# Four plain products after each piece of the first batch's attention, in a fused attention and two-layer kernel

## The chip, the cores and the metric

The kernel runs on one core of one Trainium2 chip. The metric is the device time of one execution in microseconds (us). Before the change three runs took 918.08, 918.32 and 920.32 us; the median is 918.32 us.

The engines named below are PE (TensorE, matrix products), PEld (its weight loads), DVE (VectorE), ACT (ScalarE), POOL (GpSimd) and SP (which issues the DMAs). Each engine works through its own instructions strictly in the order in which they stand.

## The reference: what is computed

```python
def _attn_ref(q, k, v):                     # 4 batches, 8 heads, 576 tokens, 64 columns
    scores = scale * np.matmul(q, k.transpose(0, 1, 3, 2))
    mask_local = (rel >= 0) & (rel < stride)                      # stride = 32, heads 0 to 3
    mask_strided = (rel >= 0) & (pos[None, :] % stride == pos[:, None] % stride)   # heads 4 to 7
    ...
    attn = np.exp(scores)
    attn = attn / (np.sum(attn, axis=-1, keepdims=True) + 1e-09)
    return np.matmul(attn, v).astype(np.float32)

def reference(**kwargs):
    attn_out = _attn_ref(**attn_kwargs)
    x = np.ascontiguousarray(attn_out.transpose(0, 2, 1, 3)).reshape(B * S, H * D)   # 2304 x 512
    x = _moe_ref(x=x, **moe_kwargs)         # g = s * relu(x @ w_in) ** 2 + b;  g @ w_out
    return _moe2_ref(x=x, **moe2_kwargs)    # g = h * cos(h), h = x @ w_in;     g @ w_out
```

Both layers go from 512 to 2048 columns and back. Their weights come as float64.

## The kernel before, in words

**Attention.** The masks leave few keys for each query, so the scores of one head fit one PSUM bank. Such a bank is an *item*. Each of the four batches has ten: four pairs of heads with two heads each ("loc" for the local heads, "str" for the strided), and two "rem" items for the tokens left over. An item passes these steps: a bf16 product of the identity with the mask puts the mask in the bank (L296), float32 products of q and k are added to it (L300), DVE takes the row maximum (L318, L319), ACT takes the exponentials (L343), DVE normalises (L356 to L358), PE transposes the result (L366), ACT copies the transposes out (L374), PE multiplies by the values (L398, two items together), and ACT and DVE write the product as two parts `xhi` and `xlo` (L109, L112).

`Attention.micro` hands this out piece by piece: values of a finished pair, transposes of the item three places back, scores of the next item. Each `next(steps)` gives one piece. `LOADS` says at which item the next operands are loaded.

**The two layers.** Every product of x with w_in and of g with w_out is three products of parts (L521, L575, L578), since the operands are split in a high and a low part. Weights are converted from float64 on DVE in small steps (`convert_ops`, L128 to L140) by `bg_step`. The first four weight tiles, `wearly`, come by DMAs that stand in the opening list of loads (`FIRST`).

**Order.** The program text is not the order on an engine. A scheduler that works at compile time puts each engine's instructions in order, with the text's order as priority: what its own reckoning takes to be ready may go ahead of what still waits. Around the change the loop is `while not att.batch_done(0)`: one piece of attention, one step of everything under way (`tick`), and 0.6 steps of weight conversion. From the third item's values on it also issues the first products of layer one.

**Banks.** PSUM has eight banks: one for "h", four for "acc", three for "att". In the first batch scores use "acc", transposes use "att" and the values' products use "h", until the first layer's products take "h" over. `dummy` is one of the three "att" banks. Before the change 18 products of zeros (L629) write it at the program's start and nothing reads it.

Of the kernel before, what the change touches and what calls it, by code (L numbers as in the profile page):

```python
# [27 lines left out]
LG, LK = 64, 96  # L28
# [18 lines left out]
ALAG = 3  # L47
# [18 lines left out]
ACT_SB = 8  # L66
PRE = 3
WARM = 18
NP0 = NC * NT - NPB * 512
PE_MASK = 2  # L70
QKW = 544
# [10 lines left out]
def net(ctx, tc, qk, vloc, vstr, w1, w2, s, b, out):  # L82
    nc = tc.nc
# [27 lines left out]
    def split_lo(dst_lo, src, hi):  # L111
        nc.vector.tensor_tensor(dst_lo, src, hi.bitcast(F32), ALU.subtract)  # L112

# [1 line left out]
    wtile, ready = {}, set()  # L115

    def convert_ops(raws, dst, key):
        """Rebias the exponent by a product, shift the top 29 + 3 mantissa bits into place, add the sign."""
        tmp = st_p.tile([P, 512], F32, tag="st", name="wtmp")
        ops = []  # L120
        o = 0
        for raw in raws:
            n = raw.shape[1]
            t = tmp[:, o : o + n]
            tu = t.bitcast(U32)
            lo32, hi32 = raw[:, :, 0], raw[:, :, 1]
            o += n
            ops.append(lambda t=t, h=hi32: nc.vector.tensor_scalar(t, h.bitcast(F32), 2.0**-112, None, ALU.mult))  # L128
            ops.append(lambda tu=tu: nc.vector.tensor_scalar(tu, tu, 3, None, ALU.logical_shift_left))
            ops.append(  # L130
                lambda tu=tu, l=lo32: nc.vector.scalar_tensor_tensor(  # L131
                    tu, l, 29, tu, ALU.logical_shift_right, ALU.bitwise_or
                )
            )
            ops.append(
                lambda tu=tu, h=hi32: nc.vector.scalar_tensor_tensor(  # L136
                    tu, h, 0x80000000, tu, ALU.bitwise_and, ALU.bitwise_or
                )
            )
        ops.append(lambda: split_hi(dst[:, 0, :], tmp))  # L140
        ops.append(lambda: split_lo(dst[:, 1, :], tmp, dst[:, 0, :]))
        ops.append(lambda: ready.add(key))
        return ops
# [16 lines left out]
    bg_due = [0.0]  # L160

    def bg_step(n):
        """Run n operations, or the fraction that is due, of the work that waits in the background."""
        bg_due[0] = min(bg_due[0] + n, 4.0)
        while bg_due[0] >= 1 and (bg_now or bg):
            if not bg_now:
                bg_now.extend(bg.pop(0)())
            bg_now.pop(0)()
            bg_due[0] -= 1

    def weight(n, k):
        """The tile, with the work that fills it issued."""
        while (n, k) not in ready:
            bg_step(1)
        return wtile[n, k]
# [5 lines left out]
            stages.append(gen)  # L181

    def tick():
        """One step of everything that is under way, the oldest first."""
        for g in list(stages):
            if next(g, "end") == "end":
                stages.remove(g)

    def w_job(n, k):
        """Loads run at once; the arithmetic follows in small steps."""  # L190
        raws = []
        for c in range(2):
            raw = st_p.tile([P, 256, 2], U32, tag="st", name="wraw")
            nc.sync.dma_start(out=raw, in_=w_src(n, k, 256 * c, 256 * (c + 1)))
            raws.append(raw)
        return convert_ops(raws, w_alloc(n, k), (n, k))

# [1 line left out]
    qk_t, v_t, rem_t = {}, {}, {}  # L199

    def load_qk(bb, hp):
# [37 lines left out]
        rem_t[bb].append(rv)  # L239

    class Item:
        """A bank of scores: `parts` are (partitions, keys, tiles, first column) and `mms` fill them."""

        def __init__(self, bb, hp, j, kind):
            self.bb, self.hp, self.j, self.kind = bb, hp, j, kind
# [14 lines left out]
                o += m * n  # L260

        def score_mms(self):
            """(partition, column, queries, keys) of each product, by part."""
            r = slice(self.j * D, (self.j + 1) * D)
            if self.kind == "rem":
                rq = rem_t[self.bb][0]
                yield 0, [(LG * hp, 0, rq[r, hp, 0, 0:LG], rq[r, hp, 1, :]) for hp in range(2)]
                res = []
                for hp in range(2):
                    rs = rem_t[self.bb][1]  # L270
                    res.append((0, LK + hp * SR, rs[r, hp, 0, :], rs[r, hp, 1, :]))
                yield 1, res
                return
            t = qk_t[self.bb, self.hp]
            res = []
            for i in range(4):
                if self.kind == "loc":
                    for g in range(2):
                        o = (2 * i + g) * LG
                        res.append((g * LG, i * LK, t[r, 0, o : o + LG], t[r, 1, o : o + LK]))  # L280
                else:
                    o = i * SG
                    res.append((0, i * SG, t[r, 0, o : o + SG], t[r, 1, o : o + SG]))
            yield 0, res
# [91 lines left out]
                    eng.tensor_copy(dst, src)  # L376

        def pv_mms(self, o):
            """Products of one head with its values; the other head of the pair fills the other columns."""
            dst = o[self.j * D : (self.j + 1) * D]  # L380
            dc = slice(self.j * D, (self.j + 1) * D)
            if self.kind == "rem":
                rv = rem_t[self.bb][2]
                res = []
                for hp in range(4):
                    m, k, c = (LG, LK, hp * LG) if hp < 2 else (SR, SR, P + (hp - 2) * SR)
                    res.append((dst[:, c : c + m], rv[:k, hp, dc], self.pt[:k, c : c + m]))
                return res
            v = v_t[self.bb, self.hp]
            m, k, n = (LG, LK, 8) if self.kind == "loc" else (SG, SG, 4)  # L390
            return [
                (dst[:, i * m : (i + 1) * m], v[:k, i, dc], self.pt[:k, i * m : (i + 1) * m]) for i in range(n)
            ]
# [39 lines left out]
        it.stored = True  # L433

    class Attention:
        """All heads' score banks in one pipeline: scores at step i, transposes at i + ALAG, values one step later."""

        def __init__(self):
            self.items = []
# [13 lines left out]
            return self.items[i] if 0 <= i < len(self.items) else None  # L453

        def batch_done(self, bb):
            """Whether the batch's last values have been written."""
            return self.items[10 * bb + 9].stored

        @property
# [1 line left out]
            return self.n > len(self.items) + ALAG  # L461

        def micro(self):
            """The pipeline's pieces: values of a pair that is done, transposes, scores."""
            while not self.done:
                i = self.n
                new, old, done = (self.item(i - k) for k in (0, ALAG, ALAG + 1))
                if done and done.j == 1:
                    while not done.moved:
                        tick()  # L470
                    spawn(run_values(self.item(i - ALAG - 2), done, self.tags[2]))
                    yield
                if old:
                    while not old.ready:
                        tick()
                    spawn(old.run_transp(self.tags[1], self.alloc))
                    yield
                if new:
                    spawn(new.run_scores(self.tags[0], new.bb < PE_MASK, self.alloc))
                bb, k = divmod(i, 10)  # L480
                for what, b_, hp in LOADS.get(k, ()):
                    if 0 < bb + b_ < B:
                        {"qk": load_qk, "v": load_v}[what](bb + b_, hp)
                if k == 9 and 0 < bb + 1 < B:
                    load_rem_qk(bb + 1)
                if k == 3 and 0 < bb < B:
                    load_rem_v(bb)
                self.n += 1
                if new:
                    yield  # L490

# [1 line left out]
    PER = NBLK * FP  # L493
    NSLOT = 2 * NPASS * PER
    h_ps, g_t, acc = {}, {}, {}
# [1 line left out]
    acc_n = [None]  # L497

    def acc_bank():
        """Two of attention's banks join the four of the accumulators when it is done."""  # L500
        if acc_n[0] is None:
            return psum("acc", "acc")
        acc_n[0] += 1
        return psum("acc" if (acc_n[0] - 1) % 6 < 4 else "att", "acc")

    def h_bank(t):
        """Attention's third bank joins the one of h."""
        return psum("h" if acc_n[0] is None or t % 2 == 0 else "att", "h_ps")

    def slot(t):  # L510
# [109 lines left out]
        )  # L620
    nc.vector.tensor_copy(identb, ident)

    # products of zeros keep the tensor engine's clock up until the first operands are there
    zeros = part[:, NP0 + (NPB - 1) * 512 : NP0 + NPB * 512 - 256]
    nc.vector.memset(zeros, 0.0)
    warm = zeros.bitcast(BF16)
    dummy = psum("att", "dummy")
# [18 lines left out]
    early = 0  # L646
    while not att.batch_done(0):
        next(steps)
        tick()
        bg_step(EARLY_BG)  # L650
        if early < 2 and att.items[PRE + 2 * early].stored:
# [99 lines left out]
```

## Time and profile before

| | |
|---|---|
| three runs, median | 918.32 us |
| profiled execution, first to last instruction (span) | 916.2 us |
| median of the runs less that span | 2.1 us |
| PE busy | 906.8 us (99%) |
| DVE busy | 581.8 us (64%) |
| ACT busy | 464.9 us (51%) |
| DMA, share of 16 engines' span | 18.5% |
| mean granted TensorE clock | 0.987 of full speed |

The profile gives the profiled execution by its span alone; what lies around the span is the 2.1 us by which the runs' median is longer. The granted clock has two levels here, 1.2 GHz (0.50) and 2.4 GHz (1.00). Times in the rows count from the span's start. A matmul's end is modelled, so neighbouring ones overlap in the timeline, and the distance between two starts says more than a duration. In the chain of waits a piece lasts from the end of the piece before it.

### The profile page before, as it was taken

How to read it: one execution, taken by the hardware profiler on the slowest of the kernel's cores; microseconds unless marked ns; L12 is line 12 of the kernel's file. 1: busy time of each engine (PE TensorE's matmuls, PEld its weight loads, DVE VectorE, ACT ScalarE, POOL GpSimd, SP SyncE). 2: the span in 40 equal slices, each digit the busy share in tenths (PEclk: the TensorE clock that was granted, in tenths of full speed). 3: DMA queues.
4: the chain of work that ended last, by engine and by line, in shares of the span. 5: the costliest groups of instructions: out<-in, count | busy, mean ns of one | idle time of the engine just before them, and what ended most of it. 6: DMA issues, size and time to landing. Idle time of an engine off the chain costs nothing.

```text
span 916.2 us, 12761 instructions
## 1 busy us (share of the span) xinstructions
PE 906.8 (99%) x4834; PEld 736.1 (80%) x4834; DVE 581.8 (64%) x1399; ACT 464.9 (51%) x1053; POOL 4.0 (0%) x15
## 2 busy tenths in 40 slices
PE   8999999999999999999999999999999999999998
PEld 4777777788888888888888888888888888888887
DVE  3598898448633883358646994479646974564444
ACT  3587977545333443344445654455445544454443
POOL 1000000000000000000000000000000000000000
PEclk8699999999999999999999999999999999999999
DMA  9446452002100230012100120013000220001111
GB/s 243 122 147 184 145 152 77 1 24 92 70 1 0 70 116 1 1 45 94 46 1 24 58 95 10 0 58 104 24 1 24 92 70 1 1 1 47 46 47 69
DMA packets 41486, 54.97 MB, mean 60 GB/s; under 512 B 7632, under 2 KB 21200, under 8 KB 41424
## 3 DMA queue, kind: packets, MB, share of 16 engines
q1 hardware_dynamic: 41424, 54.15, 18.5%
q8 instruction: 38, 0.62, 0.3%
q14 instruction: 24, 0.20, 0.1%
HBM read 49.42 MB, written 4.72 MB: 59 GB/s over the span
## 4 chain that ended last, share of the span: by engine, by line
PE 96%; DMA 2%; DVE 1%; SPq 0%; ACT 0%; issue 0%
PE h_ps L521 43%; PE acc L575 22%; PE acc L578 22%; PE s_ps L300 4%; PE o_ps L398 2%; PE t_ps L366 2%; DMA wearly<-in_w_dram 1%; PE s_ps L296 0%; DMA wraw<-in_w_dram 0%; SPq L208 0%; DVE wtmp L131 0%; DVE wtmp L128 0%; DVE wtmp L136 0%; DVE part L358 0%; SPq L219 0%; DVE part L592 0%
## 5 line engine op out<-in xcount | busy, mean ns | idle before, releaser
L521 PE MATMUL h_ps<-xhi,w 128*128 128x512 f32 (+1 forms) x1280 | 396.4, 373 | 0.6 <-DVE r L552 0.4
L521 PEld LDWEIGHTS h_ps<-xhi,w 128*128 128x128 f32 x1280 | 233.7, 188 | 45.4 <-DVE r L552 1.0
L521 PE MATMUL h_ps<-xlo,w 128*128 128x512 f32 (+1 forms) x640 | 236.1, 369 | 0.0
L575 PE MATMUL acc<-gh,w 128*128 128x512 f32 (+1 forms) x640 | 201.6, 376 | 0.0
L578 PE MATMUL acc<-w,gh 128*128 128x512 f32 x576 | 181.1, 395 | 0.0
L109 ACT ACTIVATE gh<-r 128x512 fp32r<-128x512 f32 (+1 forms) x160 | 94.1, 588 | 103.6 <-DVE r L552 52.7
L521 PEld LDWEIGHTS h_ps<-xlo,w 128*128 128x128 f32 x640 | 120.6, 188 | 21.4
L575 PEld LDWEIGHTS acc<-gh,w 128*128 128x128 f32 x640 | 116.8, 188 | 22.8 <-issue 0.7
L112 DVE TENSOR_TENSOR gl<-r,gh 128x512 fp32r<-128x512 f32 (+1 forms) x160 | 101.5, 634 | 48.1 <-ACT gh L109 42.7
L578 PEld LDWEIGHTS acc<-w,gh 128*128 128x128 f32 x576 | 107.3, 188 | 23.9 <-ACT gh L109 0.4
L575 PE MATMUL acc<-gl,w 128*128 128x512 f32 (+1 forms) x320 | 118.9, 372 | 0.0
L578 PE MATMUL acc<-w,gl 128*128 128x512 f32 x288 | 113.5, 394 | 0.0
L535 ACT ACTIVATE r<-h_ps 128x512 f32<-128x512 f32 (+1 forms) x80 | 44.1, 551 | 115.8 <-PE h_ps L521 115.4
L548 DVE SCALAR_TENSOR_TENSOR r<-a,r 128x512 f32<-128x512 f32 (+1 forms) x80 | 50.8, 635 | 71.9 <-ACT a L546 71.8
L592 DVE TENSOR_TENSOR part<-acc,part 128x512 f32<-128x512 f32 (+1 forms) x114 | 72.3, 656 | 31.9 <-PE acc L575 19.0
L541 DVE TENSOR_SCALAR r<-r,sb 128x512 f32<-128x512 f32 (+1 forms) x72 | 37.0, 514 | 80.1 <-ACT r L536 80.1
L545 ACT ACTIVATE r<-h_ps 128x512 f32<-128x512 f32 (+1 forms) x80 | 44.4, 555 | 78.6 <-PE h_ps L521 78.3
L550 ACT ACTIVATE r<-r 128x512 f32<-128x512 f32 (+1 forms) x80 | 47.2, 590 | 61.5 <-DVE r L548 61.3
L575 PEld LDWEIGHTS acc<-gl,w 128*128 128x128 f32 x320 | 60.2, 188 | 10.5
L552 DVE TENSOR_TENSOR r<-h_ps,r 128x512 f32<-128x512 f32 (+1 forms) x80 | 50.8, 634 | 27.1 <-ACT r L550 26.8
L578 PEld LDWEIGHTS acc<-w,gl 128*128 128x128 f32 x288 | 54.3, 189 | 13.0 <-DVE gl L112 0.2
L109 ACT ACTIVATE w<-wtmp 128x512 fp32r<-128x512 f32 x64 | 40.0, 626 | 24.6 <-DVE wtmp L136 20.7
(66 smaller groups left out, 776.5 us busy)
## 6 DMA issues: line engine op xcount, KB each, us to landing
wraw<-in_w_dram SPq DMA_DIRECT2D x120, 256.0 KB, 3.1
out_dram<-part SPq DMA_DIRECT2D x18, 256.0 KB, 2.0
qk<-in_qk_dram SPq DMA_DIRECT2D x8, 544.0 KB, 3.9
v<-in_vloc_dram SPq DMA_DIRECT2D x8, 384.0 KB, 4.0
qk<-in_qk_dram SPq DMA_DIRECT2D x6, 504.0 KB, 4.9
wearly<-in_w_dram SPq DMA_DIRECT2D x4, 512.0 KB
v<-in_vstr_dram SPq DMA_DIRECT2D x6, 252.0 KB
part<-in_qk_dram SPq DMA_DIRECT2D x2, 504.0 KB
```

The costliest lines, as they stand in the source:

```text
L109: nc.scalar.activation(dst_hi, src, AF.Copy)
L112: nc.vector.tensor_tensor(dst_lo, src, hi.bitcast(F32), ALU.subtract)
L521: nc.tensor.matmul(h_ps[t][:, :tb], wt[:, wi, c * P : (c + 1) * P], xt[:, c, t0 : t0 + tb], start=(c == 0 and i == 0), stop=(c == NC - 1 a ...
L535: nc.scalar.activation(r, h, AF.Relu)
L541: nc.vector.tensor_scalar(r, r, sb[:, 0:1], sb[:, 1:2], ALU.mult, ALU.add)
L545: nc.scalar.activation(r, h, AF.Copy, bias=0.25, scale=INV_2PI)
L548: nc.vector.scalar_tensor_tensor(r, a, MAGIC, r, ALU.subtract, ALU.subtract)
L550: nc.scalar.activation(r, r, AF.Sin, scale=-TWO_PI)
L552: nc.vector.tensor_tensor(r, h, r, ALU.mult)
L575: nc.tensor.matmul(o, wt[:, wi, e * P : (e + 1) * P], g, start=st, stop=sp, skip_group_check=True)
L578: nc.tensor.matmul(o, g[:, e * P : (e + 1) * P], wt[:, wi, :], start=st, stop=sp, skip_group_check=True)
L592: nc.vector.tensor_tensor(dst, o, dst, ALU.add)
```

## The change

Inside the loop of the first batch, after each piece of attention is issued, four products are added: the 128x128 bf16 identity with the 128x384 bf16 local mask, into `dummy`. `start=True` overwrites, and nothing reads the bank. 116 such products stand in the changed program. The rest of the diff takes out comments and docstrings; lines of the changed kernel are therefore one higher (L296 becomes L297) from the new constant on, and six higher behind the loop's new lines.

```diff
+KEEP = 4
...
     while not att.batch_done(0):
         next(steps)
+
+        for _ in range(KEEP):
+            nc.tensor.matmul(
+                dummy[:, : 4 * LK], identb, mloc.rearrange("p n k -> p (n k)"), start=True, stop=True, skip_group_check=True
+            )
         tick()
         bg_step(EARLY_BG)
```

The scheduler's order changes with it. On PE before the change, from the fourth item's scores to the first transposes (`s_ps` is a bank of scores, `t_ps` one of transposes; `mstr` and `part` belong to strided items):

```order
L296 LDWEIGHTS identb
L296 MATMUL s_ps<-mloc,identb 128x384
L300 MATMUL s_ps<-qk 64x96 x8
L296 LDWEIGHTS identb [waits DVE_49,Activation_49]
L296 MATMUL s_ps<-mstr,identb 126x504 [waits Pool_49]
L300 MATMUL s_ps<-part 126x126 [waits DMAHW2_49]
L300 MATMUL s_ps<-part 126x126 x3
L296 LDWEIGHTS identb [waits DVE_49]
L296 MATMUL s_ps<-mstr,identb 126x504 [waits Activation_49]
L300 MATMUL s_ps<-part 126x126 x2
L366 MATMUL t_ps<-ident,part 96x128 [waits DVE_49]
```

and the same place after it, where the fourth item's scores and one of its plain products are the last before the transposes:

```order
L297 LDWEIGHTS identb
L297 MATMUL s_ps<-mloc,identb 128x384
L301 MATMUL s_ps<-qk 64x96 x8
L652 LDWEIGHTS identb
L652 MATMUL dummy<-mloc,identb 128x384
L367 MATMUL t_ps<-ident,part 96x128 [waits DVE_49,Activation_49]
```

The strided items' scores, of which one and a half stood ahead of the first transposes, now stand behind the second; 17 plain products stand ahead of the first transposes, 99 behind them.

On DVE before, from the first item's maximum to its normalised scores (`sm` holds maxima and sums, `wtmp` is a weight tile in conversion):

```order
L318 TENSOR_REDUCE sm<-s_ps 128x4 [waits PE_49]
L319 TENSOR_SCALAR sm<-sm 128x4 [waits DVE_49]
L318 TENSOR_REDUCE sm<-s_ps 128x4 [waits PE_49]
L319 TENSOR_SCALAR sm<-sm 128x4 [waits DVE_49]
L318 TENSOR_REDUCE sm<-s_ps 128x4 [waits PE_49]
L319 TENSOR_SCALAR sm<-sm 128x4 [waits DVE_49]
L318 TENSOR_REDUCE sm<-s_ps 128x4 [waits PE_49]
L128 TENSOR_SCALAR wtmp<-wearly 128x512 [waits DMAHW6_49]
L356 TENSOR_SCALAR sm<-sm 128x4 [waits Activation_49]
```

and after:

```order
L319 TENSOR_REDUCE sm<-s_ps 128x4 [waits PE_49]
L320 TENSOR_SCALAR sm<-sm 128x4 [waits DVE_49]
L319 TENSOR_REDUCE sm<-s_ps 128x4 [waits PE_49]
L320 TENSOR_SCALAR sm<-sm 128x4 [waits DVE_49]
L129 TENSOR_SCALAR wtmp<-wearly 128x512 [waits DMAHW6_49]
L319 TENSOR_REDUCE sm<-s_ps 128x4 [waits PE_49]
L357 TENSOR_SCALAR sm<-sm 128x4 [waits Activation_49]
```

The first step of weight conversion, which waits for a DMA, has moved ahead of the third item's maximum.

## Rows read from the trace of the kernel before

**Rows 1.** The page: busy time of three engines with its share and instructions, and the granted clock in 40 slices of 22.9 us, in tenths.

```profile
PE 906.8 (99%) x4834; PEld 736.1 (80%) x4834; DVE 581.8 (64%) x1399; ACT 464.9 (51%) x1053; POOL 4.0 (0%) x15
...
PEclk8699999999999999999999999999999999999999
```

**Rows 2.** Busy time by stretch: from and to, length, then busy us (instructions) of PE, PEld, DVE, ACT and POOL, the granted clock, the DMA share and GB/s.

```profile
7.24:14.49 7.25, 6.84 (x83) 4.77 (x81) 2.74 (x7) 5.21 (x25) 0.00 (x0) 1.00 1.13 283
14.49:17.42 2.93, 0.01 (x2) 0.00 (x1) 2.16 (x9) 0.47 (x3) 0.00 (x0) 0.73 1.15 242
17.42:39.70 22.28, 22.28 (x133) 15.91 (x133) 11.36 (x37) 9.91 (x41) 0.00 (x0) 0.50 0.55 163
39.70:50.00 10.30, 10.25 (x118) 7.25 (x116) 7.92 (x33) 8.87 (x41) 0.00 (x0) 1.00 0.25 67
50.00:60.00 10.00, 9.19 (x90) 6.86 (x90) 9.50 (x33) 8.54 (x38) 0.00 (x0) 1.00 0.58 177
60.00:160.00 100.00, 100.00 (x830) 75.94 (x830) 88.22 (x290) 79.16 (x274) 0.00 (x0) 1.00 0.47 141
```

**Rows 3.** Who waited for whom from 60 us to the end, PE alone: waiter, releaser, us in total, times, longest.

```profile
PE h_ps L521 <- DVE r L552: 0.4, 1, 0.4
```

**Rows 4.** The chain of waits around the first transposes: start, us, what.

```profile
4.87 10.37 DMA wearly<-in_w_dram
15.26 0.43 DVE wtmp L128
15.69 0.08 DVE sm L356
15.84 0.33 DVE wtmp L129
16.17 0.09 DVE sm L357
16.25 0.64 DVE wtmp L131
16.89 0.48 DVE part L358
17.42 1.09 PE t_ps L366 x4
```

**Rows 5.** Timeline: PE and its weight loads in the warm-up of 18 products of 512 columns (start, us, engine, line, instruction, count).

```profile
1.19 6.22 PE L629 MATMUL dummy<-part 128*128 128x512 bf16 x18 [1.19 <-DVE part L625]
...
5.00 0.15 PEld L629 LDWEIGHTS <-part 128*128 128x128 bf16 x1 [0.28 <-issue]
5.43 0.15 PEld L629 LDWEIGHTS <-part 128*128 128x128 bf16 x1 [0.28 <-issue]
5.73 1.18 PEld L629 LDWEIGHTS <-part 128*128 128x128 bf16 x6 [0.15 <-issue]
```

**Rows 6.** The chain of waits, pieces of one kind at the low clock (before 39 us) and at the full one.

```profile
20.97 1.02 PE t_ps L366 x4
24.55 1.90 PE o_ps L398 x30
29.20 1.14 PE s_ps L300 x4
...
46.48 0.27 PE s_ps L296
47.80 0.16 PE s_ps L296
57.26 0.57 PE t_ps L366 x4
59.19 1.07 PE s_ps L300 x8
65.08 1.07 PE o_ps L398 x30
```

**Rows 7.** Timeline of PE: local scores of two items, the first strided ones, and plain 512-column products of layer one with what follows them.

```profile
8.31 0.34 PE L296 MATMUL s_ps<-mloc,identb 128*128 128x384 bf16 x1
9.38 0.34 PE L296 MATMUL s_ps<-mloc,identb 128*128 128x384 bf16 x1
12.01 0.43 PE L296 MATMUL s_ps<-mstr,identb 126*126 126x504 bf16 x1 [0.41 <-ACT part L343]
...
41.37 0.40 PE L521 MATMUL h_ps<-xhi,w 128*128 128x512 f32 x1
41.69 1.08 PE L398 MATMUL o_ps<-part 126*64 126x126 f32 x14
43.27 0.39 PE L521 MATMUL h_ps<-xhi,w 128*128 128x512 f32 x1
43.50 0.59 PE L366 MATMUL t_ps<-ident,part 126*126 126x126 f32 x4
```

**Rows 8.** Timeline of DVE: a maximum of a local item, and the conversion's first step with the wait ahead of it.

```profile
10.57 0.56 DVE L318 TENSOR_REDUCE sm<-s_ps 128x4 f32<-128x384 f32 x1 [0.32 <-PE s_ps L300]
15.26 0.43 DVE L128 TENSOR_SCALAR wtmp<-wearly 128x512 f32<-128x512 f32 x1 [3.06 <-DMA wearly<-in_w_dram]
```

**Rows 9.** Who waited for whom from 7 to 60 us, the weight loads that wait for nothing shown.

```profile
PEld s_ps L300 <- issue: 5.2, 18, 0.5
```

## The prediction

> **What bounds the kernel now.** I read the busy times first [rows 1]: PE is busy for 99% of the span, and no other engine comes near. Then the stretches [rows 2]: from 60 us on PE has no idle time to speak of; the one wait from there to the end is 0.4 us [rows 3]. So PE is the bound, and whatever its first 60 us lose or gain arrives at the end unchanged. The clock line [rows 1] shows one weak spot, in its first two slices. The stretches place it [rows 2]: PE stands idle from 14.49 to 17.42 us, the granted clock falls from 1.00 to 0.50 in that gap (mean 0.73), and it stays at 0.50, the 1.2 GHz level, to 39.70 us although PE is busy all that time. It is 1.00 afterwards. Pieces of one kind say what the low clock costs [rows 6]: 30 value products took 1.90 us against 1.07, four score products 1.14 against half of 1.07, four transposes 1.02 against 0.57. That is a factor of 1.8 to 2.1; I use 2. The chain of waits [rows 4] says why PE stood idle: the first transposes wait for DVE's normalising, and DVE had been held until 15.26 us by the conversion's first step, which waited for the DMA of `wearly`.
>
> What the change can win back is therefore bounded. PE's idle time between 7.24 and 60 us is 0.41 + 2.92 + 0.05 + 0.81 = 4.2 us, and the low clock costs half of 22.28 us, which is 11.1 us [rows 2]. Together 15.3 us; if all of it went and the new products were free, the time would be 903.
>
> **What it adds: 116 plain products.** The trace has no repeated product of 384 columns, so I take the warm-up's [rows 5]: at full clock six weight loads of 512-column products lie within 1.18 us, and less the last load's own 0.10 us that is five distances of 0.216 us from start to start; at the low clock it is 0.43 us (5.00 to 5.43). The loads lie beside the products. For 384 columns that makes three quarters, 0.16 us at full and 0.32 us at low clock. The lone 384-column product of the mask took 0.16 us and 0.27 us in the chain [rows 6]; 0.27 is my upper bound, 0.16 my value, as the repeats are alike and nothing is loaded between them but the same identity. A lower bound is a product absorbed in the gaps of its neighbours: float32 score loads wait 5.2 us for nothing shown [rows 9], 18 times, so a few tens of ns might be had at each of 29 groups; 1 us in all. Sum: 116 x 0.162 = 18.8 us at full clock, bounds 18 and 31.
>
> Leaving a full-width product may cost something. A 512-column product of layer one is followed after 0.32 us by values' products, but after 0.23 us by transposes [rows 7]. So there is 0.1 us at the five value pieces, nothing at transposes, and the mask's own product already pays this at scores: 0.5 us, bounds 0 and 2.
>
> **The wait before the first transposes stays.** Local scores take 1.07 us an item [rows 7]. PE starts them at 7.24, so four items and 17 plain products end at 7.24 + 4.3 + 2.8 = 14.3 us. What releases the transposes is DVE's chain behind the `wearly` DMA [rows 4], in which nothing is faster now: the conversion's step has even moved ahead of the third item's maximum, a 0.56 us operation [rows 8] that had been done before the DMA landed and now comes after it. The DMAs ahead of `wearly` stand as they did, so I keep 15.26 us for its landing and expect the transposes at 17.42 + 0.5 = 17.9 us. PE then idles 3.6 us. Behind the waiting transposes on PE stand seven plain products and all later scores; ACT and DVE get nothing new meanwhile. The 17 products are thus not free: they stand where one and a half strided items (12.01 to 14.49 us, some 2.1 us of work [rows 2, 7]) stood before, and that work now comes after the gap.
>
> **The clock.** With a gap at least as long as before, it falls again. Then the order matters: the transposes are followed by seven full-width products, and in every piece after that four of them take 1.3 us of low-clock time beside 1 to 2 us of other work. How soon the clock returns is shown by two rises. In the warm-up it rose about 4.5 us after the first plain product (1.19 to about 5.7 us [rows 5]); in the attention, without them, only after 22 us. I take the first: low from 17.9 to about 22.7 us, a loss of half of 4.8, or 2.4 us. Bounds: 0 if the clock never falls, and for a return only near 31 us half of 13, or 6.5.
>
> The Trainium skill bears on this (TensorE: Matmul & The Clock Gate, Part 4: PE-mode transpose): transposes do not count as busy work for the clock as plain products do. The trace agrees as far as it goes, for PE was full from 17.42 to 39.70 at clock 0.50 [rows 2], partly with transposes. By it the added products would be what brings the clock back, which changes nothing in the sum.
>
> **What else could be late.** The dummy bank keeps one of the three "att" banks, so transposes go round two; between an item's transposes and those two items on stand some 20 plain products and four to six other pieces, 6 us of PE work or more, against one copy on ACT. I count 0. DVE and ACT have 11.4 and 9.9 us of work in the 22.28 us stretch [rows 2]; the changed stage is longer in time than before, not shorter, so neither becomes the bound and the 0.81 us of idle time after 50 us should go. Bounds 0 and 2.
>
> **Sum.** After, overhead on PE: 18.8 + 0.5 + 3.6 + 2.4 = 25.3 us. Before: 15.3 us. The profiled execution goes from 916.2 to 926.2 us; with the 2.1 us that lie around the span the median goes from 918.3 to 928.4 us. The products cost more than everything that they could restore.
>
> **Rivals.**
> - *The clock returns late.* For it: half or more of each piece is still 64-row or transposed work, in which the clock stayed low for 22 us [rows 2]. Against it: the seven full-width products in one run, right after the gap. Return at 31 us costs 6.5 instead of 2.4: 932.5 us. No return until the last plain product would be far worse: about 24 us of work at full clock (11.1 from the low stretch, 2.1 of strided scores, 11 between 39.7 and 51 us) plus 99 x 0.162 = 16 us, all at half speed, gives 40 us instead of 2.4, near 966.
> - *The clock never falls.* The plain products run to within 3.6 us of the transposes. For it: they are heavier work than the strided scores that stood there. Against it: the gap is longer than the one that cost the clock before. It gives 918.3 + 18.8 + 0.5 + 3.6 - 15.3 = 926 us.
> - *The other side: the products are absorbed.* PE is drawn as busy through its float32 pieces, but a modelled end hides gaps between load and product [rows 9]. If a plain product slipped into such gaps and cost little, the change would win. With 6.0 us of wait and low clock left, it breaks even at (15.3 - 6.0 - 0.5) / 116 = 0.076 us a product, half of its 384 columns at the warm-up's rate; at 0.05 us the time is 915.3. Against it: each product occupies PE for its columns, and none of the rows shows one faster than that.
> - *A cheaper product.* The Trainium skill (same page, Back-to-back issue gap) gives a sustained 131 ns for 512 columns and 81 ns for 128. The trace disagrees: 0.21 us for 512 columns in the warm-up [rows 5]. An estimate between its two figures is 0.114 us for 384 columns.
>   As a mechanism of this kernel, products that overlap their neighbours by a third of their columns cost 0.108 us each instead of 0.162, together 12.5 us, and give 922.1 us.
>
> **How the numbers follow.** My forecast, 928.4 us, has 0.65. A late return has 0.15, and no return until the end of the batch 0.03. A clock that never falls has 0.09. Cheaper products at 922.1 have 0.04, absorbed ones 0.04. A measurement of this kernel tells 0.3%, or 2.8 us, from no change. All cases but the absorbed ones lie above 921.1, so slower has 0.95; of the remaining 0.05 I give 0.03 to no change and 0.02 to faster. The range runs from 923 (the low bounds of product and clock together, with some absorption) to 936 (a late return with 0.19 us a product), which leaves out the absorbed products, the full upper bound of 0.27 us, and the case without return.
>
> **What would show it.** Right: the new products' group lasts 0.16 us from start to start; PE waits 3 to 4 us for DVE before the first transposes, and DVE 4 to 5 us for `wearly`; the stretch with clock 0.50 ends by 25 us; from 60 us on PE is full as before. Wrong: a transposes' wait under 2 us, a clock that stays up or stays down, new products nearer to 0.1 or 0.27 us, or PE idle for more than 2 us between 25 and 62 us, which would be a wait that I priced at nothing.

## The result, and the profile after

The changed kernel takes 924.89 us (median of four runs, 923.77 to 926.24) against 919.32 us for the kernel before in the same comparison (four runs, 918.08 to 920.46). The ratio is 1.0056, with an interval of 1.004 to 1.0073: the change makes the kernel about 5.6 us slower. The time lies within the range, 3.5 us below the forecast of 928.4. The profiled execution's span is 923.4 us against 916.2, which is 7.2 us. The kernel before differs from run to run by the length of its low-clock stretch (its mean clock goes from 0.983 to 0.994), and the execution whose profile is shown is 1.2 us shorter than the median (918.08 us), while the changed one's is 0.3 us longer (925.20 us). That makes up the 1.6 us between the two differences.

The page of the changed kernel, in the two lines that answer to [rows 1]:

```profile
PE 913.4 (99%) x4950; PEld 739.5 (80%) x4950; DVE 585.0 (63%) x1399; ACT 466.1 (50%) x1053; POOL 4.0 (0%) x15
...
PEclk9999999999999999999999999999999999999999
```

The 8 and the 6 at the start of the clock line are gone, yet PE is busy for 6.6 us more, with 116 more instructions. Busy time by stretch of the changed kernel (from and to, length, busy us and instructions of PE, PEld, DVE, ACT and POOL, granted clock, DMA share, GB/s), which answers to [rows 2]:

```profile
7.24:14.30 7.06, 6.75 (x84) 4.23 (x80) 1.46 (x4) 3.97 (x17) 0.00 (x0) 1.00 1.13 267
14.00:18.65 4.65, 0.00 (x0) 0.03 (x1) 2.65 (x10) 1.11 (x7) 0.00 (x0) 0.96 1.08 246
18.25:21.66 3.41, 3.01 (x11) 1.90 (x12) 3.33 (x11) 2.60 (x13) 0.00 (x0) 0.50 0.84 227
21.70:58.00 36.30, 36.30 (x355) 25.41 (x354) 32.41 (x108) 22.12 (x90) 0.00 (x0) 1.00 0.56 169
60.00:160.00 100.00, 100.00 (x857) 75.98 (x852) 78.02 (x251) 76.88 (x273) 0.00 (x0) 1.00 0.43 128
```

In this execution the gap is longer than before, 4.65 us against 2.93. The clock falls in it, at 18.25 us, and is back at 21.66 us instead of 39.70. From there PE has no idle time for 36 us, where before it lost 0.81 us between 50 and 60 us. Who waited for whom in the changed kernel up to 60 us, one line of DVE and two of PE (waiter, releaser, us in total, times, longest):

```profile
DVE wtmp L129 <- DMA wearly<-in_w_dram: 5.6, 1, 5.6
...
PE t_ps L367 <- DVE sm L357: 4.7, 1, 4.7
PE h_ps L522 <- ACT xhi L110: 0.5, 1, 0.5
```

The first two are the stall of [rows 2, 8], longer by 2.5 and 1.8 us. The change alone does not make it longer: in the second profile of the same kernel (e8 below) the same wait of PE is shorter than before.

```profile
PE t_ps L367 <- DVE sm L357: 2.1, 1, 2.1
```

There DVE's first conversion step begins at 14.70 us, here at 16.00. The chain of waits of the changed kernel (start, us, what) shows the gap's end and what comes behind it:

```profile
5.77 10.21 DMA wearly<-in_w_dram
...
16.00 0.43 DVE wtmp L129
16.43 0.47 DVE sm L319
...
18.65 1.06 PE t_ps L367 x4
19.71 2.16 PE dummy L652 x7
21.87 0.44 PE t_ps L367 x4
...
24.35 1.08 PE o_ps L399 x32
25.43 0.76 PE dummy L652 x4
26.19 0.44 PE t_ps L367 x4
26.63 0.65 PE dummy L652 x4
```

The third item's maximum (0.47 us) now stands between the DMA's landing and the normalising, as its place in the order says. The first transposes still run at the low clock (1.06 us); the seven plain products behind them take twice their time (2.16 us, 0.31 each), and the next transposes are at full speed. One of these rows differs from [rows 6] at the same clock: 32 value products in one run take 1.08 us, where 30 took 1.07 and the other two stood apart. The 0.44 us of the transposes against the 0.57 of [rows 6] is no such gain, since the chain measures between modelled ends. The timeline of PE before (start, us, engine, line, instruction, count) shows the transposes of that row:

```profile
57.19 0.64 PE L366 MATMUL t_ps<-ident,part 128*96 128x128 f32 x4
57.58 0.47 PE L521 MATMUL h_ps<-xhi,w 128*128 128x512 f32 x1
```

From start to start they took 0.39 us ahead of a 512-column product. The timeline of the changed kernel gives the same distances for its products:

```profile
7.82 0.82 PE L652 MATMUL dummy<-mloc,identb 128*128 128x384 bf16 x4
8.48 0.33 PE L297 MATMUL s_ps<-mloc,identb 128*128 128x384 bf16 x1
...
26.46 0.81 PE L652 MATMUL dummy<-mloc,identb 128*128 128x384 bf16 x4
27.11 0.38 PE L297 MATMUL s_ps<-mstr,identb 126*126 126x504 bf16 x1
```

Four plain products take 0.66 us in the first place and 0.65 us in the second, 0.16 us each.

**One account for all kernels.** From its first scores to 4.0 us before the end PE sets the time, so the span can be split by PE alone (those 4.0 us are left out of the table). Each PE instruction gets the time from its start to the start of the next, less the idle time before that next one. Time at the low clock is counted half for its instruction, the other half as "low clock". The half is an assumption: the pieces of [rows 6] give factors of 1.8 to 2.1, which could move up to 1.2 us between "low clock" and attention's work where the clock was low for 22 us. Sums in us, profiled executions (e8 is the changed kernel once more; its account is within 0.2 us of it but for a start 1.3 us later and 2.5 us less idle time):

| | before | after | e1 | e2 | e3 | e4 | e5 | e6 | e7 | e9 | e10 |
|---|---|---|---|---|---|---|---|---|---|---|---|
| up to the first scores | 7.2 | 6.8 | 7.0 | 7.9 | 6.6 | 6.8 | 7.4 | 7.2 | 7.7 | 7.6 | 6.6 |
| plain products | 0 | 19.7 | 9.8 | 4.8 | 3.3 | 0 | 19.5 | 0 | 0 | 5.4 | 2.7 |
| PE idle | 4.6 | 5.2 | 3.5 | 3.3 | 5.5 | 2.9 | 1.5 | 7.2 | 6.4 | 0.3 | 1.6 |
| low clock | 11.2 | 1.5 | 1.7 | 3.3 | 5.3 | 3.3 | 0 | 5.0 | 11.2 | 0 | 1.6 |
| attention's scores, transposes, values | 79.5 | 76.2 | 77.6 | 77.9 | 78.5 | 81.6 | 76.5 | 77.9 | 76.6 | 79.6 | 81.2 |
| the two layers | 809.7 | 810.0 | 810.1 | 810.0 | 809.9 | 809.7 | 809.5 | 810.2 | 810.3 | 810.5 | 809.3 |
| span | 916.2 | 923.4 | 913.7 | 911.2 | 913.2 | 908.3 | 918.4 | 911.6 | 916.1 | 907.3 | 907.1 |
| attention's groups on PE, whole run | 150 | 136 | 141 | 140 | 143 | 150 | 136 | 137 | 138 | 146 | 148 |

The last row counts the lines of scores, transposes and values in the timeline, where neighbouring instructions of one kind are one line. It goes over the whole run, in which every kernel has the same 1072 products of attention. After less before: products +19.7, low clock −9.6, attention's own work −3.2, idle time +0.6, the start −0.5, the layers +0.3; together +7.2 us. The layers differ by up to 1.2 us between these executions, so terms of half a microsecond say little.

### The profile page after: what moved, and what is told of

Read it like the earlier page. It is cut to its first block, busy times and chain, and to the rows that moved or that the text cites. A ratio compares the mean times of both kernels' runs of the same rounds, so it can differ in the third digit from the quotient of the medians.

```text
span 923.4 us, 12983 instructions
## 1 busy us (share of the span) xinstructions
PE 913.4 (99%) x4950; PEld 739.5 (80%) x4950; DVE 585.0 (63%) x1399; ACT 466.1 (50%) x1053; POOL 4.0 (0%) x15
## 3 DMA queue, kind: packets, MB, share of 16 engines
q1 hardware_dynamic: 41424, 54.15, 18.8%
## 4 chain that ended last, share of the span: by engine, by line
PE 96%; DMA 1%; DVE 1%; SPq 1%; ACT 0%; issue 0%; ACTq 0%
PE h_ps L522 44%; PE acc L576 22%; PE acc L579 22%; PE s_ps L301 3%; PE o_ps L399 2%; PE t_ps L367 2%; PE dummy L652 1%; DMA wearly<-in_w_dram 1%; DMA wraw<-in_w_dram 0%; PE s_ps L297 0%; SPq L209 0%; SPq L220 0%; DVE wtmp L132 0%; DVE sm L319 0%; ACT part L344 0%; DVE part L593 0%
## 5 line engine op out<-in xcount | busy, mean ns | idle before, releaser
L546 ACT ACTIVATE r<-h_ps 128x512 f32<-128x512 f32 (+1 forms) x80 | 44.4, 555 | 78.4 <-PE h_ps L522 78.1
L576 PEld LDWEIGHTS acc<-gl,w 128*128 128x128 f32 x320 | 60.2, 188 | 10.6 <-issue 0.2
```

Source lines behind the costliest of these rows:

```text
L546: nc.scalar.activation(r, h, AF.Copy, bias=0.25, scale=INV_2PI)
L576: nc.tensor.matmul(o, wt[:, wi, e * P : (e + 1) * P], g, start=st, stop=sp, skip_group_check=True)
```

## The experiments

`tc.issue_after(x)` keeps what is issued in it behind x in the scheduler's order; it adds no work. All edits are to the kernel before unless said, and are shown shortened (`...`).

**e1: two products after each piece** (58 in all).

```diff
         next(steps)
+        for _ in range(2): nc.tensor.matmul(dummy...)   # the changed kernel's product
```

> Two plain products after each piece (58 in all) instead of four. Theory A (each plain product costs its 0.16 us on TensorE, and what brings the clock back is the handful right after the gap): the low stretch still ends by about 22 us, and the time is 924.9 - 58 x 0.163 = 915.4 us, below before's 919.3. Theory B (the dense share of the whole stage holds the clock up): with half the density the low stretch lasts far beyond 25 us, and the time stays within 3 us of 924.9. Theory C (the time lost comes from the new order and its longer wait for DVE, the products are nearly free): about 924.

Measured: 914.51 us against 920.54, ratio 0.9943 (0.9929 to 0.9957). The windows of e1:

```profile
18.00:22.20 4.20, 3.95 (x17) 2.33 (x17) 4.17 (x15) 2.73 (x12) 0.00 (x0) 0.60 0.82 239
22.20:60.00 37.80, 37.80 (x387) 27.32 (x386) 32.45 (x108) 28.72 (x115) 0.00 (x0) 1.00 0.57 161
```

Half the products bring the clock back as soon (22.2 us) and cost half (9.8 us). The sign of the change turns on their number. Products are paid for one by one, and two of the four at each piece bought nothing.

**e2: one product after each piece** (29 in all).

```diff
         next(steps)
+        for _ in range(1): nc.tensor.matmul(dummy...)
```

> One plain product after each piece (29 in all). Theory A, if a few in one place suffice: 924.9 - 87 x 0.163 = 910.7 us. If one a piece is too thin to bring the clock back, it stays low to about 40 us as before, and the time is 919.3 plus 29 x 0.16 to 0.32 less what lies in the gap, 922 to 927 us. Theory C: about 924.

Measured: 913.29 us, ratio 0.993 (0.9917 to 0.9943). The windows of e2:

```profile
17.20:24.00 6.80, 6.62 (x36) 4.99 (x37) 4.27 (x17) 3.95 (x18) 0.00 (x0) 0.50 0.77 244
24.00:60.00 36.00, 34.60 (x381) 25.76 (x380) 30.89 (x102) 28.05 (x114) 0.00 (x0) 1.00 0.52 148
```

The low stretch is now 6.8 us long, where e1's began at 18.8 us and lasted 3.4. The saving on products against e1 is 5.0 us; in the account 1.6 us of it go to low clock and 0.9 to a later start, and by the medians e2 gains only 1.2 us on e1.

**e3: 20 products, only behind the gap.** With fewer products, the question is whether those that stand right behind the gap are enough.

```diff
+        if 4 <= piece <= 8:
+            with tc.issue_after(att.items[0].t_ins):   # the first item's last transpose
+                for _ in range(4): nc.tensor.matmul(dummy...)
```

> Only 20 plain products, tied behind the first transposes (the end of the gap), none elsewhere. The wait before the transposes is that of before (2.9 us) and the order ahead of it too. Theory A: the clock falls in the gap, is back by 21 to 23 us and then stays up without further plain products; gain 12 us of the low stretch less 2 us that stay, cost 20 x 0.163 = 3.3 us: 919.3 - 10 + 3.3 = 912 to 913 us, faster than both kernels. Theory B: without plain products the clock falls again or never returns, and the time is 919.3 + 3.3 to 6 = 922 to 926 us.

Measured: 918.70 us (twelve runs, 915.03 to 919.11), ratio 0.9985 (0.9968 to 1.0002): not told from no change. The profiled execution is the fastest of the twelve; its windows and one wait of its PE:

```profile
16.00:21.40 5.40, 4.33 (x17) 2.84 (x18) 4.40 (x14) 1.92 (x10) 0.00 (x0) 0.50 0.96 255
21.40:45.30 23.90, 22.49 (x240) 16.29 (x238) 18.36 (x63) 17.66 (x73) 0.00 (x0) 1.00 0.56 163
45.30:52.10 6.80, 6.29 (x42) 4.70 (x43) 5.54 (x19) 4.08 (x21) 0.00 (x0) 0.50 0.18 42
```

```profile
PE t_ps L366 <- ACT part L343: 1.4, 1, 1.4
```

The 20 products do bring the clock back by 21.4 us, and the attention's own work, with six products of layer one in it from 31 us on, keeps it up for 24 us. It falls again at 45.3 us, within a wait of 1.4 us (44.4 to 45.8 us). My expectation took the clock, once back, for safe. That explains part of the 6 us by which it was missed: the second low stretch costs 3.4 us in the profiled execution, which is itself 3.7 us below the median. Eight of the twelve executions have a lower mean clock (0.989 against 0.992); where theirs was low no trace shows.

**e4: no gap.** The conversion's first step is moved behind the third item's normalising on DVE, and nothing is added on PE.

```diff
-        bg_step(EARLY_BG)
+        if att.items[2].ready:
+            with tc.issue_after(att.items[2].n_ins.ins):   # its normalising on DVE
+                bg_step(EARLY_BG)
```

> No plain products; the weight conversion's steps are tied on DVE behind the third item's normalising, so that DVE no longer waits for the weight DMA ahead of the first items. Theory D (the idle gap alone throws the clock down): TensorE's wait of 2.9 us goes, the granted clock stays at 1.00, and 2.9 + 12 us are won: 904 to 906 us. Rival E (the thin float32 work alone lets the clock fall, gap or no gap): the clock is low from about 16 us to 35 us or more, and only the wait goes: 916 to 918 us.

Measured: 909.02 us (four runs, 908.01 to 910.05), ratio 0.9883 (0.9868 to 0.9898), some 11 us faster than before. The windows of e4, and what its PE waited for (up to 62 us):

```profile
14.00:26.25 12.25, 12.25 (x136) 9.32 (x136) 11.11 (x36) 10.65 (x48) 0.00 (x0) 1.00 0.81 223
18.00:38.70 20.70, 19.18 (x214) 13.48 (x208) 16.69 (x59) 14.66 (x62) 0.00 (x0) 1.00 0.78 212
38.70:45.60 6.90, 6.67 (x32) 4.87 (x32) 4.59 (x16) 4.09 (x23) 0.00 (x0) 0.51 0.48 135
```

```profile
PE s_ps L300 <- DMA qk<-in_qk_dram: 1.2, 1, 1.2
PE h_ps L523 <- ACT xhi L109: 0.5, 1, 0.5
```

Between 14 and 38.7 us the clock is 1.00 without one plain product. Up to 26.3 us PE has attention's work alone, the kind that left the clock at 0.50 before [rows 2], and no idle time; from there to 38.7 us six 512-column products of layer one (L523) stand in it, which in the kernel before began only at 40.8 us. With the idle gap gone the clock did not fall there: the gap is what cost it, and the rival, that this work alone lets it fall from about 16 us, is excluded. The wait of 1.2 us in the rows (27.0 to 28.2 us) left the clock up, while it fell at 38.7 us within the wait of 0.5 us. In two of the four runs the mean clock is 1.00 (908.0 and 908.5 us), in the other two it is 0.996 (909.5 and 910.1 us, the latter profiled). I had expected 904 to 906; the account says where the rest went: 3.3 us of that late low clock, and attention's work that is 2.1 us dearer than before. The timeline of e4's PE shows the second:

```profile
15.61 0.33 PE L400 MATMUL o_ps<-part,v 96*64 96x64 f32 x2
15.87 1.14 PE L300 MATMUL s_ps<-part 64*126 64x126 f32 x8
16.94 0.64 PE L368 MATMUL t_ps<-ident,part 128*96 128x128 f32 x4
17.51 1.15 PE L400 MATMUL o_ps<-part,v 96*64 96x64 f32 x30
```

A piece of 32 value products is cut: two, then another item's scores and transposes, then thirty. The two take 0.26 us from start to start, where 32 whole ones take no longer than the thirty (1.08 us in the chain above). This is a cut that the changed kernel does not have.

**e5: no gap, and four products after each piece.** e4's edit, and the change's:

```diff
         next(steps)
+        for _ in range(4): nc.tensor.matmul(dummy...)
...
+            with tc.issue_after(att.items[2].n_ins.ins):
+                bg_step(EARLY_BG)
```

> The tied weight conversion of e4_no_gap together with the four plain products after every piece (116): the clock should be up in both kernels where it matters, so the difference to e4's 909.0 us is the bare price of the products. Theory A (each takes its 0.163 us, 18.9 us in all; the clock's late fall of e4, worth 3.4 us, goes; the pieces, no longer cut up, are some 4 us cheaper): 920 to 921 us. Without an effect of uncut pieces: 924 to 925 us. If the products were absorbed in gaps: 906 to 909 us.

Measured: 920.80 us, ratio 1.0022 (1.0004 to 1.004). In the profiled execution the clock is 1.00 until the last 1.1 us of the span, though PE waits once as long as in e3:

```profile
PE h_ps L523 <- ACT xhi L109: 1.4, 1, 1.4
```

In two of the ten runs the mean clock is 0.996 and 0.994 (923.3 and 926.8 us), so even with four products after each piece it was low for some microseconds; no trace shows where. A window and three rows of the timeline of e5's PE:

```profile
26.00:40.00 14.00, 14.00 (x130) 9.65 (x128) 12.59 (x42) 9.64 (x39) 0.00 (x0) 1.00 0.62 167
```

```profile
20.63 0.60 PE L368 MATMUL t_ps<-ident,part 128*96 128x128 f32 x4
21.07 0.81 PE L652 MATMUL dummy<-mloc,identb 128*128 128x384 bf16 x4
21.72 0.38 PE L296 MATMUL s_ps<-mstr,identb 126*126 126x504 bf16 x1
```

With nothing left to restore, the products cost 19.5 us, 0.168 each; four transposes ahead of them take 0.44 us. The span exceeds e4's by 10.1 us only, because low clock (3.3), idle time (1.4) and attention's work (5.1) are less. The expectation held.

**e6 and e7: the pieces kept whole, without products.** In the changed kernel attention's work costs 3.2 us less. If that is because its pieces are not cut, the same order by force should give it for nothing. e6 has it on top of e4, e7 on the kernel before.

```diff
+        last = [x for x in nc.cur_bb.bb.instructions if x.engine == mybir.EngineType.PE][-1]
+        if piece >= 12:
+            with tc.issue_after(last):
+                next(steps)
```

> e4_no_gap with TensorE's pieces from the twelfth on held in the order of the program text, so that none is cut up by another; no plain products. Theory F (cut pieces pay at every change of tile shape, some 4 us at full clock over the first batch): 909.0 - 4 = 905 us, less if the late fall of the clock goes too. Theory G (the scheduler's cutting fills waits, and without it TensorE waits for DVE and ACT as long): 908 to 911 us with new waits on TensorE.

> The kernel before with its pieces from the twelfth on held in the order of the text; the gap, the weight conversion's place and the clock's fall stay as they were, no plain products. Theory F: the order is worth 4 us at full clock and more at the low one, so 912 to 916 us against before's 919 to 920.5, with the low stretch as long as before. Theory G: no gain, 919 us or more. Theory H (the change wins only by the clock): as G.

Measured: e6 914.20 us, ratio 0.9944 (0.9926 to 0.9963), worse than e4; e7 918.96 us, ratio 0.9998 (0.9972 to 1.0025), no change. The work does become cheaper, by 3.7 us against e4 and 2.9 us against before. But PE now waits more (7.2 us in e6 against e4's 2.9, and 6.4 in e7 against 4.6). Two lines from e6's waits up to 62 us:

```profile
PE h_ps L523 <- DVE xlo L112: 3.3, 2, 3.0
...
PE t_ps L368 <- DVE part L358: 1.0, 2, 0.6
```

and the stretch of its longest wait:

```profile
22.00:26.00 4.00, 1.29 (x28) 0.99 (x22) 4.00 (x13) 2.50 (x11) 0.00 (x0) 1.00 0.50 147
```

At the end of this idle time e6's clock falls for 10 us (26.1 to 36.3). For e7 the same views:

```profile
PE t_ps L366 <- DVE part L358: 2.2, 1, 2.2
...
PE h_ps L521 <- DVE xlo L112: 1.1, 1, 1.1
```

```profile
18.00:40.00 22.00, 20.87 (x137) 15.98 (x137) 14.99 (x42) 13.16 (x55) 0.00 (x0) 0.50 0.60 182
```

Its clock stays low as before's does. The reading that fits is that the scheduler cuts pieces to cover waits: without the cuts the waits are open, and the gain on cuts is given back.

**e8: the changed kernel again**, to put it on the scale of the later comparisons.

> The changed kernel once more, beside the others on the same chip: 924 to 926 us. With e1 (58 products) and e2 (29) it gives the price of a product where the clock returns alike: theory A 0.163 us each between 58 and 116, so 914.5 + 9.4 = 924; absorbed: below 918.

Measured: 925.11 us (924.07 to 926.05), ratio 1.0068 (1.0045 to 1.0091), as the first time.

**e9 and e10: towards the best.** e9 is e4 with one product after each piece; e10 is e4 with two after each piece from the 22nd on (16 in all), meant for the place where e4's clock may fall.

```diff
+        for _ in range(1): nc.tensor.matmul(dummy...)                        # e9
...
+        for _ in range(2 if piece >= 22 else 0): nc.tensor.matmul(dummy...)  # e10
```

> e4_no_gap with one plain product after every piece (29 in all). Theory A and F together: 29 x 0.168 = 4.9 us more, less the late fall of the clock (0 to 3.3 us) and up to 3 us from pieces that are cut up less: 907 to 911 us, beside e4's 909.0. If the products were free: 903 to 905.

> e4_no_gap with two plain products after each piece from the 22nd on only (16 in all), where e4's clock fell late, at 38.7 us. Theory A: 16 x 0.168 = 2.7 us more, and the late fall (3.3 us in the runs that have it) gone in all: 907.5 to 909.5 us, with clock 1.00 in every run. If the late fall stays: 911 to 912 us.

Measured: e9 909.15 us (908.34 to 909.37), ratio 0.989 (0.985 to 0.993), and e10 910.19 us (ten runs, 908.66 to 913.68), ratio 0.9903 (0.9879 to 0.9926). One window of e9:

```profile
18.00:40.00 22.00, 22.00 (x222) 15.06 (x224) 17.11 (x60) 14.89 (x64) 0.00 (x0) 1.00 0.74 206
```

and of e10 a window and a wait of PE:

```profile
40.00:50.00 10.00, 8.47 (x75) 6.22 (x72) 7.56 (x27) 7.75 (x36) 0.00 (x0) 0.83 0.44 131
```

```profile
PE h_ps L523 <- ACT xhi L109: 1.5, 1, 1.5
```

In e9 PE has no idle time in that stretch and the mean clock is 1.00 in all four runs, but the 29 products cost 5.4 us, as much as they save: e9 equals e4 and is only steadier, in four runs of each. In e10's profiled execution the clock still falls, at 41.9 us, within a wait of 1.5 us (40.6 to 42.1). But e10 did not try what it was meant to: nothing tied its products to their place, and the scheduler put five of the 16 at 10.9 to 11.6 us and none behind 37.4 us. In the other nine runs the mean clock (0.994 to 0.998) shows only that it was low somewhere. e4 and e9 are the best versions, 10 to 11 us below the kernel before by their ratios and 16 below the changed one.

## Why the prediction was right, and where it was off

The direction and the range held, and the chain of reasons was mostly the one that acted.

- *The products cost PE their columns.* Forecast 0.162 us each, 18.8 in all, and 0.5 for leaving a full-width product. Measured 0.162 to 0.163 from start to start within most groups, and 19.7 us in the account with what follows, 0.170 each. e1, e2 and e5 give 0.168, 0.164 and 0.168 each, whether or not there was anything to restore; e9's 29 cost 0.185 each. This excludes the rivals of absorbed (0.05) and of cheaper products (0.108). By the Trainium skill (TensorE: Matmul & The Clock Gate, Back-to-back issue gap) a product of N columns that stands alone is spaced by N/2.4 + 2.5 ns, an estimate of 162.5 ns for 384; the trace agrees with this figure, not with the page's lower one for a sustained stream.
- *The wait stays; its size is not settled.* Forecast 3.6 us with PE's transposes at 17.9; measured 4.67 us and 18.65 in one profile, and 2.07 us and 17.35 in the other of the same kernel (e8). In the first PE was done with its scores and products a little early (14.0 instead of 14.3 us). DVE's first conversion step, which shows the landing of `wearly` that I had kept at 15.26 us, began at 16.0 and at 14.7 us. The cause of that spread stays open; that the forecast lies between the two is partly luck.
- *The clock falls and comes back early.* Forecast low to about 22.7 us, a loss of 2.4 us; measured to 21.66, a loss of 1.5. The products did this: the low stretch lasts 3.4 us with four and with two a piece, 6.8 us with one (e2), and 24 us without (e7, 16.7 to 40.6 us). The forecast start of 17.9 us and the 4.5 us of the warm-up give an end at 22.4, not 22.7 us, a slip worth 0.15 us of the loss. The rivals of a late return and of a clock that never falls are excluded by the windows.
- *What could be won back.* I put 15.3 us at stake, 4.2 of idle time and 11.1 of low clock; the account has 4.6 and 11.2 for the whole run. Of these 5.2 and 1.5 are left; of the idle time after 50 us, which I expected to go, 0.5 us stayed. In e8 2.7 and 1.7 are left.

By the overhead that I listed, the span should have risen by 10.0 us, and that part of the account gives 19.7 + 5.2 + 1.5 − 4.6 − 11.2 = 10.6 us. **The step that failed is the one that kept attention's own work at its old price:** "What else could be late" asked only for new waits and put 0 to 2 us there, and no term of the sum allowed the remaining pieces to become cheaper. They did, by 3.2 us (79.5 to 76.2). The count of attention's groups falls with the added products, 150 to 136 over the whole run, and 150 to 136 again from e4 to e5. The likely reason, which no run tries by itself, is that products that are always ready give the scheduler something to put into a wait, so it does not cut one item's piece for another. That the order carries the price is shown by e7, where forced order alone takes 2.9 us off the same work with no plain product and the same low clock. Over all eleven kernels the cost falls with the count, by an estimate of 0.3 us a group (a straight line through the table), but the count is not all of it: the kernel before and e4 both have 150 groups, at 79.5 and 81.6 us. What within a cut costs the time was not separated. The earlier start of the first scores (−0.5) and the layers (+0.3) make up the rest of the 7.2 us. Between span and median I counted 2.1 us; the profiled execution had 1.8, and lay 0.3 above its median.

The reading of the cause was right but not used far enough. The profile showed that one DVE instruction, early in its queue and waiting for a DMA, made the gap. The change leaves it there and pays 19.7 us to repair 9.6 us of low clock; e4 moves the instruction, adds no work on PE, and keeps the clock up to 38.7 us.

## What to carry to other kernels

When a clock has dropped, look first for the wait behind which it dropped, and move the instruction that holds the queue: here that was worth 11 us, and filler at four a piece lost 5.6. Where filler is used, count it by its columns on the bounding engine and give only as much as brings the clock back. Look at the order on the engine for where it went: e10's filler was not where its wait was. And when ready work is added under a scheduler, compare the order of the old work too, since its own price can change.

## What the runs showed that I had not expected

- Attention's float32 work alone ran for 12 us at clock 1.00 when it began there (e4, 14.0 to 26.25 us, PE full) and for 22 us at 0.50 when it began there (before, 17.42 to 39.70 us, PE full). With plain products among it, clock 1.00 returned within 3 us of the first transposes (after, 18.65 to 21.66 us), 4 us in e1 and 7 us in e2.
- Once back, the clock was not safe, and the length of a wait does not say whether it falls. It fell within waits of 1.4 us (e3), 1.5 us (e10) and 0.5 us (e4). It stayed up through waits of 1.2 us (e4, at 28 us), 1.4 us (e5, up to 54.6 us, and e2, up to 50.2 us) and 0.5 us (the changed kernel, at 58 us). What decides between these was not tried. The wait of e2:

```profile
PE t_ps L366 <- DVE sm L356: 1.4, 1, 1.4
```

- The order in which attention's pieces stand has a price: with 136 to 150 groups the same 1072 products took 76.2 to 81.6 us.
